# Attention scores in two one-bank tiles, and three banks in place of four for transposes

## The chip, the cores and the metric

The kernel runs on one core of one Trainium2 chip. The metric is the time in microseconds on the device for one execution, the median of several runs. Engines are named as the profile names them: PE is TensorE's matmul side and PEld its weight loads, DVE is VectorE, ACT is ScalarE, POOL is GpSimd, SP is SyncE, whose queue issues most transfers. [...]

## What is computed

Sparse attention, and behind it a routed layer of eight experts on its output. Of the eight heads, the first four look back over 32 positions (local), the last four at positions of the same remainder by 32 (strided). Cut to what matters:

```python
def _attn_ref(q, k, v):                 # 8 batches, 8 heads, 576 positions, 64 wide
    scores = scale * np.matmul(q, k.transpose(0, 1, 3, 2))
    mask_local = (rel >= 0) & (rel < stride)
    mask_strided = (rel >= 0) & (pos[None, :] % stride == pos[:, None] % stride)
    scores = np.where(masks[None, :, :, :], scores, -1000000000.0)
    scores = scores - np.max(scores, axis=-1, keepdims=True)
    attn = np.exp(scores)
    attn = attn / (np.sum(attn, axis=-1, keepdims=True) + 1e-09)
    return np.matmul(attn, v)

def _moe_ref(x, w_skip, w_gate, w1, w2):   # x: attention output, 4608 rows of 512
    do_compute = x @ w_skip > 0
    e_idx = np.argmax(x @ w_gate, axis=1)  # for the rows with do_compute
    y = gate_w * (np.maximum(x @ w1[e], 0.0) @ w2[e])
    out = x + y where do_compute, else x
```

All inputs and the output are float32.

## The kernel before

**Stages.** The first part, up to about 178 us, is the attention of all batches, with the routing of each finished batch woven in. The second part is the expert layers: weights are loaded and split in two parts, rows are gathered, and three matmuls stand for each float32 product. The second part opens PSUM pools of its own; the edit touches only the pool of the first.

**Units.** A batch is four units of attention (`UNITS`): two local ones of 5 and 4 blocks (64 queries against 96 keys each) and two strided ones of 6 and 5 blocks (54 queries against 54 keys, in tiles of 64). Two pairs of heads, j = 0 and 1, are done together, and each pair's two heads lie in the lower and upper 64 partitions, i = 0 and 1. A score matmul takes 64 rows of the array and writes 64 partitions, so the four combinations of i and j use the four 64x64 tiles of the array: row half i, column half i xor j.

**The steps of a unit.** `qk` (line 189) multiplies the scores into a tile tagged "S" (line 199), DVE adds the mask into an SBUF buffer `sm` (line 206 local, 208 strided), takes the maxima (214), and POOL subtracts them, one instruction for each j (217). The two strided units share one `sm` buffer. `tex` (222) transposes the result on PE in groups of up to four into a bank tagged "T" (237), and ACT's Exp copies each group out (245). `pv` (251) multiplies by the values into a two-bank tile "PV" (271), and DVE normalises (279 to 286). `xpose` (304) transposes the unit's output in groups of four into T banks (313), and ACT copies them to `xT` (315). There is one `xT` buffer for each kind of head, shared by all batches.

**The routing of a batch.** `score` (325) multiplies `xT` with the router's weights in two halves, each in a T bank (329), which ACT empties with two copies (333, 334). `route1` (337) transposes that into a T bank (349), and DVE works out the choice; `route2` (396) counts ranks in a T bank (400 to 406), read at 411; `place` (452) multiplies one-hot matrices into a T bank (456), read at 460 or 462.

**What sets the order.** One loop over the 32 units (line 848). In visit n it runs the scores of unit n + 2, then the transposes of unit n's exponentials, pv of unit n - 1, and the output transposes of unit n - 2. The orders of PE, DVE and POOL in this loop are those of the program text (`manual_schedule`, line 847); ACT and the transfers are ordered by the framework's scheduler. In the visit of a batch's first strided unit the loop puts `xpose` of the same batch's first local unit ahead of pv, and after pv come `score` half 0, `score` half 1 of the batch before, and then `tex` (lines 874 and 903). In the visit of the next batch's first local unit come `tex`, pv, `route2`, `xpose`, and `place` (lines 887 to 908).

**PSUM.** The pool of the first part gives out eight banks by tag: S one tile of two banks, T four tiles of one, PV one tile of two. A tile is given out anew when the instructions that read it are through.

## Time and profile before

| | us |
|---|---|
| median of 3 runs | 451.05 |
| lowest and highest | 447.95, 451.74 |
| the profiled execution, its own time | 453.04 |
| its span, first to last instruction | 451.3 |
| mean granted TensorE clock in it | 0.976 |

The profile is of one execution, so sums over its rows are to be held against 453.04 and not against the median. A row of the timeline gives start and length in us, engine, line, operation, the tiles out and in, the shape, and in brackets how long the engine sat idle before it and what ended that. A row may stand for several instructions (x40); a matmul in float32 makes two records. PE's records overlap, since matmuls are pipelined, so a row's length is the start times of its matmuls and the length of the last.

### The profile page before, as it was taken

The numbers are of one execution on the slowest core, as the hardware profiler recorded it, in microseconds if no ns is written. First come the engines' busy times: TensorE is split into PE (matmuls) and PEld (weight loads), VectorE is DVE, ScalarE is ACT, GpSimd is POOL, SyncE is SP. The second block draws the span as 40 slices with busy tenths as digits, with TensorE's granted clock in tenths as the row PEclk, the third lists the DMA queues.
The fourth block names the chain that finished last, engine by engine and source line by source line (L and its number), as shares of the span: only waits on it lengthen the run. The fifth ranks groups of instructions, "written<-read, shape, count | busy, mean of one in ns | idle before, by whom it ended". The sixth has DMA issues, their size and how long they took to land.

```text
span 451.3 us, 12196 instructions
## 1 busy us (share of the span) xinstructions
PE 412.4 (91%) x4991; PEld 370.0 (82%) x4992; DVE 280.9 (62%) x606; ACT 186.4 (41%) x370; POOL 142.6 (32%) x200
## 2 busy tenths in 40 slices
PE   5989899799889667999899999999999999999994
PEld 3866768587677556789799799999999999999984
DVE  2666798969987876781377465365484564755611
ACT  1334443436345316642443243444444444544400
POOL 2434445344454355034014327012224023200201
PEclk9799999999989979999999999999999999999999
DMA  8999989979893134515347466546566466655201
GB/s 287 388 393 315 350 276 343 326 227 352 265 377 120 43 101 153 172 69 141 91 155 212 155 201 205 167 153 187 187 199 186 152 209 192 210 159 169 61 20 42
DMA packets 51805, 90.38 MB, mean 200 GB/s; under 512 B 8251, under 2 KB 27963, under 8 KB 51745
## 3 DMA queue, kind: packets, MB, share of 16 engines
q1 hardware_dynamic: 45249, 79.19, 52.8%
q0 software_dynamic: 6496, 10.37, 8.0%
q8 instruction: 40, 0.66, 0.6%
q14 instruction: 20, 0.16, 0.1%
HBM read 75.16 MB, written 14.91 MB: 200 GB/s over the span
## 4 chain that ended last, share of the span: by engine, by line
PE 50%; DMA 2%; POOL 0%; DVE 0%; POOLq 0%; issue 0%
PE S L652 15%; PE S L654 15%; PE S L653 15%; PE PV L744 2%; DMA xg<-out_dram,tab 2%; PE T L646 1%; PE PV L786 0%; PE PV L784 0%; PE PV L785 0%; PE S L760 0%; PE S L759 0%; PE S L761 0%; POOL out_dram L732 0%; PE T L771 0%; PE S L646 0%; PE PV L646 0%
## 5 line engine op out<-in xcount | busy, mean ns | idle before, releaser
L652 PE MATMUL S<-xh,w1h 128*128 128x342 f32 (+6 forms) x248 | 78.6, 317 | 0.2 <-DVE hl L665 0.2
L654 PE MATMUL S<-xh,w1l 128*128 128x342 f32 (+6 forms) x248 | 76.7, 309 | 0.0
L653 PE MATMUL S<-xl,w1h 128*128 128x342 f32 (+6 forms) x248 | 76.6, 309 | 0.0
L732 POOL DMA_INDIRECT out_dram<-ot,tab x25 | 28.0, 1122 | 150.0 <-DVE ot L730 141.8
L652 PE MATMUL S<-hh,w2h 128*128 128x288 f32 (+5 forms) x192 | 59.4, 310 | 0.5 <-DVE hl L665 0.5
L654 PE MATMUL S<-hh,w2l 128*128 128x288 f32 (+5 forms) x192 | 58.0, 302 | 0.0
L653 PE MATMUL S<-hl,w2h 128*128 128x288 f32 (+5 forms) x192 | 57.9, 302 | 0.0
L664 ACT ACTIVATE hh<-S 128x342 fp32r<-128x342 f32 (+6 forms) x64 | 28.0, 437 | 64.0 <-PE S L654 58.3
L588 DVE TENSOR_TENSOR w1l<-raw,w1h 128x1024 fp32r<-128x1024 f32 x32 | 39.0, 1223 | 20.0 <-ACT w1h L582 20.0
L199 PE MATMUL S<-kt,qt 64*64 64x54 f32 (+1 forms) x1280 | 34.3, 247 | 14.9 <-DVE sms L208 5.0
L652 PEld LDWEIGHTS S<-xh,w1h 128*128 128x128 f32 x248 | 46.9, 189 | 0.9 <-issue 0.4
L653 PEld LDWEIGHTS S<-xl,w1h 128*128 128x128 f32 x248 | 46.8, 189 | 0.1
L654 PEld LDWEIGHTS S<-xh,w1l 128*128 128x128 f32 x248 | 46.7, 188 | 0.0
L199 PEld LDWEIGHTS S<-kt,qt 64*64 64x64 f32 x1280 | 28.3, 145 | 22.2 <-issue 7.3
L217 POOL TENSOR_TENSOR sm<-sm,mx 128x480 f32<-128x480 f32 (+1 forms) x32 | 28.5, 911 | 55.8 <-DVE mx L214 29.3
L624 POOL DMA_INDIRECT xg<-out_dram,tab x25 | 33.7, 1347 | 36.8 <-issue 14.4
L588 DVE TENSOR_TENSOR w2l<-raw,w2h 128x1024 fp32r<-128x1024 f32 x32 | 39.1, 1223 | 9.8 <-ACT w2h L582 9.6
L665 DVE SCALAR_TENSOR_TENSOR hl<-S,hh 128x342 fp32r<-128x342 f32 (+6 forms) x64 | 30.9, 483 | 17.8 <-ACT hh L664 17.7
L652 PEld LDWEIGHTS S<-hh,w2h 128*128 128x128 f32 x192 | 36.1, 188 | 0.8 <-DVE hl L665 0.8
L315 ACT COPY xT<-T 128x512 f32<-128x512 f32 (+4 forms) x56 | 22.2, 441 | 35.0 <-PE T L313 34.8
L649 DVE TENSOR_TENSOR xl<-T,xh 128x288 fp32r<-128x288 f32 (+7 forms) x30 | 13.1, 468 | 37.3 <-ACT xh L648 37.2
L653 PEld LDWEIGHTS S<-hl,w2h 128*128 128x128 f32 x192 | 36.3, 189 | 0.0
(180 smaller groups left out, 828.3 us busy)
## 6 DMA issues: line engine op xcount, KB each, us to landing
raw<-in_w_dram SPq DMA_DIRECT2D x64, 512.0 KB
vt<-in_vp_dram SPq DMA_DIRECT2D x40, 390.0 KB
qt<-in_qp_dram SPq DMA_DIRECT2D x16, 304.0 KB
kt<-in_kp_dram SPq DMA_DIRECT2D x16, 297.0 KB
out_dram<-x SPq DMA_DIRECT2D x16, 288.0 KB
kt<-in_kp_dram SPq DMA_DIRECT2D x14, 304.0 KB
qt<-in_qp_dram SPq DMA_DIRECT2D x14, 288.0 KB
out_dram<-x SPq DMA_DIRECT2D x32, 99.0 KB
```

The source lines that it names most:

```text
L199: T.matmul(s[HP * (i ^ j):HP * (i ^ j) + HP, j, (blk - b0) * win:(blk - b0 + 1) * win], lhsT=qt[p, j, blk * nq:blk * nq + HP], rhs=kt[p, j ...
L217: G.tensor_tensor(e[:, j], sw[:, j], mx[:, j].unsqueeze(2).broadcast_to([128, b1 - b0, win]), op=ALU.subtract)
L315: A.copy(xT_[b, kind][:, :, g * nq:(g + m) * nq].rearrange("p i (n q) -> p n i q", q=nq), t[:, 0:m * 128].rearrange("p (n i q) -> p n i q" ...
L588: V.tensor_tensor(lo, raw_.pop((key, j)), hi.bitcast(F32), op=ALU.subtract)
L624: i = G.indirect_dma_start(out=xg[:s["P"], t, :], out_offset=None, in_=out[0:last, :], in_offset=bass.IndirectOffsetOnAxis(ap=s["tab"][:s[ ...
L649: V.tensor_tensor(xl[:, c, :C], t[:, :C], xh[:, c, :C].bitcast(F32), op=ALU.subtract)
L652: T.matmul(p, lhsT=a[0], rhs=b[0], start=start, stop=False)
L653: T.matmul(p, lhsT=a[0], rhs=b[1], start=False, stop=False)
L654: T.matmul(p, lhsT=a[1], rhs=b[0], start=False, stop=stop)
L664: A.activation(s["hh"][:, f, :C], p[:, :C], AF.Relu)
L665: V.scalar_tensor_tensor(s["hl"][:, f, :C], p[:, :C], 0.0, s["hh"][:, f, :C].bitcast(F32), op0=ALU.max, op1=ALU.subtract)
L732: i = G.indirect_dma_start(out=out, in_=ot[:P], in_offset=None, bounds_check=NTOK - 1, oob_is_err=False, out_offset=bass.IndirectOffsetOnA ...
```

## The change

The score tile of two banks becomes two tiles of one bank, taken one after the other from three that carry the tag S; T has three banks in place of four. The loop over the matmuls is turned round: first all blocks for j = 0, then all for j = 1. The mask is added by two instructions, one for each tile, each half as long. What follows (maxima, subtraction, and all else) is as it was, and so is the number of matmuls.

```diff
-    psum, bufs = pctx.enter_context(tc.tile_pool(name="psum", bufs=1, space=PSUM)), {"S": 1, "T": 4, "PV": 1}
+    psum, bufs = pctx.enter_context(tc.tile_pool(name="psum", bufs=1, space=PSUM)), {"S": 3, "T": 3, "PV": 1}
...
-        s = ps("S", 2)
-        for blk in range(b0, b1):
-            for j in range(2):
+        s = [None, None]
+        for j in range(2):
+            s[j] = ps("S")
+            for blk in range(b0, b1):
                 for i in range(2):
                     p = slice(HP * i, HP * i + HP)
-                    T.matmul(s[HP * (i ^ j):HP * (i ^ j) + HP, j, (blk - b0) * win:(blk - b0 + 1) * win],
+                    T.matmul(s[j][HP * (i ^ j):HP * (i ^ j) + HP, (blk - b0) * win:(blk - b0 + 1) * win],
                              lhsT=qt[p, j, blk * nq:blk * nq + HP], rhs=kt[p, j, blk * nq:blk * nq + win],
                              start=True, stop=True)
         yield
         sm = sms[pr][:, :, 0:n]
-        if kind == 0:
-            mask = con["ml"][:, (b0 > 0) * LW:(b0 > 0) * LW + n]
-            V.tensor_tensor(sm, s[:, :, 0:n], mask.unsqueeze(1).broadcast_to([128, 2, n]), op=ALU.add)
-        else:
-            V.tensor_tensor(sm.rearrange("p j (n w) -> p j n w", w=win),
-                            s[:, :, 0:n].rearrange("p j (n w) -> p j n w", w=win),
-                            con["ms"].unsqueeze(1).unsqueeze(1).broadcast_to([128, 2, b1 - b0, win]), op=ALU.add)
+        for j in range(2):
+            if kind == 0:
+                mask = con["ml"][:, (b0 > 0) * LW:(b0 > 0) * LW + n]
+                V.tensor_tensor(sm[:, j], s[j][:, 0:n], mask, op=ALU.add)
+            else:
+                V.tensor_tensor(sm[:, j].rearrange("p (n w) -> p n w", w=win),
+                                s[j][:, 0:n].rearrange("p (n w) -> p n w", w=win),
+                                con["ms"].unsqueeze(1).broadcast_to([128, b1 - b0, win]), op=ALU.add)
```

## The prediction

> **What bounds the kernel now.** I read the page first (busy shares, slices, the chain that ended last), then the windows view of the attention part, then the waits, and then the timeline where the edited tiles are used.

> ```profile
> span 451.3 us, 12196 instructions
> PE 412.4 (91%) x4991; PEld 370.0 (82%) x4992; DVE 280.9 (62%) x606; ACT 186.4 (41%) x370; POOL 142.6 (32%) x200
> PE   5989899799889667999899999999999999999994
> DVE  2666798969987876781377465365484564755611
> DMA  8999989979893134515347466546566466655201
> PE 50%; DMA 2%; POOL 0%; DVE 0%; POOLq 0%; issue 0%
> ...
> 20.00:147.00 127.00, 113.65 (x2514) 90.78 (x2506) 101.95 (x267) 57.84 (x136) 56.23 (x98) 0.97 0.90 306
> ```

> The last row is the windows view from 20 to 147 us: busy time of PE, PEld, DVE, ACT and POOL, then the granted clock, the DMA share and GB/s. PE is busy 113.65 of 127 us, so it idles 13.4 us; DVE is busy 80%, ACT 46%, and the DMA engines 0.90. The chain that ended last runs on PE. What delays PE in the attention part (about the first 178 us) therefore delays the end, unless a later wait takes the delay up. Nothing after that part uses the edited pools. The profiled execution took 453.04 us (span 451.3, 1.7 around it); the median shown is 451.05, 2.0 lower. I sum on 453.04 and take 2.0 off.

> **What the third score bank can give.** In the old kernel the scores of the next unit cannot start before the mask of the last one has emptied the only buffer. These are PE's waits for it, in total and at their places:

> ```profile
> PE S L199 <- DVE sms L208: 5.0, 5, 1.8
> PE S L199 <- DVE sm L206: 2.1, 2, 1.1
> PE S L199 <- DMA kt<-in_kp_dram: 3.9, 5, 2.6
> ...
> 11.62 0.46 PE L199 MATMUL S<-kt,qt 64*64 64x54 f32 x4 [1.06 <-DVE sm L206]
> 12.33 1.53 PE L199 MATMUL S<-kt,qt 64*64 64x54 f32 x44 [0.25 <-DMA kt<-in_kp_dram]
> ...
> 51.64 0.38 PE L199 MATMUL S<-kt,qt 64*64 64x54 f32 x9 [0.68 <-DVE sms L208]
> 56.35 0.41 PE L199 MATMUL S<-kt,qt 64*64 64x96 f32 x6 [0.68 <-DVE sms L208]
> 112.12 0.80 PE L199 MATMUL S<-kt,qt 64*64 64x54 f32 x40 [0.43 <-DVE sms L208]
> 117.58 0.41 PE L199 MATMUL S<-kt,qt 64*64 64x96 f32 x4 [1.46 <-DVE sms L208]
> 151.01 0.27 PE L199 MATMUL S<-kt,qt 64*64 64x54 f32 x2 [1.00 <-DVE sm L206]
> 157.35 0.34 PE L199 MATMUL S<-kt,qt 64*64 64x54 f32 x8 [1.78 <-DVE sms L208]
> 164.07 0.36 PE L456 MATMUL T<-hpm,hlo 128*128 128x120 bf16 x2 [3.58 <-POOL hpm L446]
> ```

> With three one-bank tiles a unit's first tile always finds a bank that the unit before last has left, and its second needs only the first half of the last unit's mask. I let all mask waits go: 7.1 us by the first two rows. Of these 0.68 + 0.68 + 0.43 + 1.46 = 3.25 lie where PE goes on afterwards. The 1.00 and 1.78 do not count: at 164.07 PE waits 3.58 us more, for a POOL product at the end of a chain of DVE and POOL work, so an earlier PE only waits longer there. The 1.06 at 11.62 I cost at nothing: a load of kt is late next, at 12.33. The gain is 3.3 us; its ends are 0 and 7.1.

> **What the fourth transpose bank was worth: the two score products of the router.** Once a batch (first visit of its strided half), PE does in order: two groups of transposes of the new outputs (L313), pv, `score` half 0, `score` half 1 (L329), then `tex` (L237). Each group and each half takes a bank of T:

> ```profile
> 76.95 0.74 PE L313 MATMUL T<-cs,x 128*128 128x128 f32 x5
> 78.61 2.11 PE L329 MATMUL T<-xT,w 128*64 128x288 f32 x16
> 79.85 0.39 ACT L333 COPY s<-T 32x288 f32<-32x288 f32 x1 [3.29 <-PE T L329]
> 80.26 0.65 ACT L334 COPY s<-T 32x288 f32<-32x288 f32 x1
> 80.93 0.76 ACT L315 COPY xT<-T 128x512 f32<-128x512 f32 x2
> 81.01 1.00 PE L237 MATMUL T<-cs,frame 128*118 128x128 f32 x6 [0.29 <-issue]
> ```

> The copies of the transposes (L315) do not run when the transposes are done at 77.69, although ACT then sits idle for 3.29 us: they write `xT`, of which there is one buffer, and `score` of the batch before still reads it. So two banks stay held until both halves are multiplied. With four banks the halves take the other two, and only `tex` waits: it starts at 81.01, just behind half 0's copies (80.91). With three, half 1 has no bank left and waits itself for those copies. Half 0 takes half of the 16 records' start times, about 0.9 us, so half 1 could start at 79.5 and starts at 81.0: 1.45 us. Then all three banks hang on half 1. Its first `xT` copy can follow about 1.24 us after its start (78.61 to 79.85 is the same distance), at 82.2, and takes some 0.52 of the 0.76 for two; `tex` starts at 82.75 in place of 81.01. That is 1.74 us, less 0.1 that the second `tex` group waits today: 1.65 us. This happens for six batches alike (the seventh runs its halves before its transposes: 0.5 us). The sum is 6 x 1.65 + 0.5 = 10.4 us. Below, if `tex` is not hurt again, 6 x 1.45 less today's wait of 0.5 each = 5.7; above, if ACT does half 1's copies (0.39 + 0.65) before the `xT` copies, 6 x 2.4 = 14.4. Nothing covers it: PE's order is written out by hand, and the next unit's scores stand behind `tex`.

> **The placing product.** The second place where four banks are in use at once:

> ```profile
> 70.62 0.19 PE L400 MATMUL T<-rohb,tri 128*128 128x40 bf16 x1
> 70.78 0.85 PE L313 MATMUL T<-cs,x 128*128 128x128 f32 x6
> 71.47 0.43 PE L456 MATMUL T<-hpm,hlo 128*128 128x120 bf16 x5
> 71.51 0.76 ACT L315 COPY xT<-T 128x432 f32<-128x432 f32 x2 [0.88 <-PE T L313]
> 71.83 0.80 PE L199 MATMUL S<-kt,qt 64*64 64x54 f32 x40
> 72.09 0.19 DVE L411 TENSOR_TENSOR rdd<-T,rohb 128x40 f32<-128x40 f32 x1
> ```

> The ranks (L400) hold a bank until DVE reads them at 72.09, the two groups of L313 hold two, and `place` (L456) needs a fourth at 71.47. With three it waits for the first copy, which ends near 72.05: 0.6 us, in four batches, 2.4 us (ends 0 and 4 x 0.8 for the read at 72.28). Elsewhere (the `tex` groups of a local unit, `route1`) I find three banks enough: a bank is copied out before its third successor starts.

> **The new order of the score matmuls.** The old loop visits all four 64x64 tiles of the array in every block; the new one does all blocks on two tiles (j = 0), then all on the other two. Each matmul makes two records.

> ```profile
> 69.77 0.92 PE L271 MATMUL PV<-vt,pts 54*64 54x65 f32 x40
> ...
> 95.52 1.39 PE L271 MATMUL PV<-vt,ptl 96*64 96x65 f32 x40
> 97.53 1.06 PE L199 MATMUL S<-kt,qt 64*64 64x96 f32 x40
> ```

> Taking off a last matmul of 0.22 to 0.24 us, the old order gives one record in 21 ns (96 columns) and, by the row at 71.83, in 15 ns (54 columns). If only two tiles ran at a time it would be about 42 and 30 ns; the local pv, which has only two tiles, shows 30 ns at 65 columns. That costs 0.83 + 0.67 + 0.70 + 0.58 = 2.8 us a batch, 22 us in all. But the strided pv (69.77) also orders its work by pairs, four matmuls on the two tiles of one half of the rows and then four on those of the other, and still runs at 18 ns: PE started the other tiles while earlier work of the first two was pending. So the order need not be kept between tiles, over at least four matmuls. Here the distance is 8 to 12. Ends: 0 and 22 us. I take 1.6 us (0.05 for each of 32 units, the time to step over the first tile's work), because the pv row is the nearest.

> [...]

> **The split mask.** One DVE instruction becomes two of half the length.

> ```profile
> L206 DVE TENSOR_TENSOR sm<-S,cs 128x960 f32<-128x960 f32 x8 | 9.2, 1150 | 6.7 <-DMA cs<-in_cst_dram 6.4 <-PE S L199 0.3
> L206 DVE TENSOR_TENSOR sm<-S,cs 128x768 f32<-128x768 f32 x8 | 7.6, 951 | 2.2 <-PE S L199 2.2
> L208 DVE TENSOR_TENSOR sms<-S,cs 128x540 f32<-128x540 f32 x8 | 5.7, 714 | 9.8 <-POOL frame L217 8.3 <-PE T L313 1.5
> ```

> From 768 to 960 elements costs 199 ns, so about 155 ns of each are fixed: 32 more of them are 5.0 us of DVE. In 20 to 147 us DVE has 25 us idle, which hides it; behind a mask stand the normalising of pv, the maxima and POOL's subtraction. Where DVE is late already (147 to 164 us), four units pay 0.15 each: 0.6 us, ends 0 and 5. Against it, the masks that wait for POOL (8.3 us in the last row, off PE's path) can now start their first half after POOL's first subtraction; I cost that at nothing.

> **The sum**: -3.3 + 10.4 + 2.4 + 1.6 + 0.6 = +11.7 us. Of PE's 13.4 us of idle time, waits that the profile calls "issue" and loads can shrink when PE comes later; I take 1.7 off for them. 453.04 + 10.0 = 463.0, and for the median 461.

> **The rivals.**
> 1. Two tiles at a time (strict order): 22 in place of 1.6 us: 481; with a view ahead that covers half of it, 470. For it: nothing here shows a distance of 8 to 12. Against it: the row at 69.77. Chance 0.12 for the full price, 0.10 for half.
> 2. Something else paces the attention part, so that the bank waits fill idle time that was there anyway: 13.4 us of it, as much as the sum. For it: the DMA share of 0.90. Against it: PE waits only 3.9 us for kt loads, in five places. Time: 451 to 452. Chance 0.16.
> 3. Faster: half 1 of `score` does not wait, because the `xT` copies can be done before it. The 10.4 then becomes 0 (and today's 0.5 a batch goes too, 3.0), and the mask waits decide: 451 - 7.1 - 3.0 + 2.4 + 1.6 + 0.6 = 445.5. It decides if the copies of L315 start before the second half of L329. Against it: ACT's idle 3.29 us. Chance 0.08.

> **How the numbers follow.** My forecast has chance 0.54, its own range 455 to 468: the ends of the `score` term (5.7, 14.4) and of the gain (0, 7.1). The range of all is 450 to 476: it takes in rival 2 and half the price of rival 1 and leaves out rival 3 and the full price. Within 1% (446.5 to 455.6) is what a measurement of this kernel can hardly tell from no change. Faster: 0.08. Same: rival 2 and 0.04 of the forecast's lower end, 0.20. Slower: 0.72.

> **What would show it.** Right: the 16 records of L329 split in two eights about 1.45 us apart, PE waiting for ACT's L334 between them, and `tex` (L237) some 4.2 us after the start of L329 (2.4 now); no wait of L199 for L206 or L208; score runs of 40 records near 0.85 and 1.1 us; L456 behind the first L315. Wrong: runs of 1.4 to 1.9 us (rival 1); PE idle in 20 to 147 us unchanged and the same span (rival 2); L315 ahead of the second half of L329 (rival 3).

## The result, and the profile after

The changed kernel takes 466.6 us (median of 4 runs, 465.1 to 469.0) beside 450.5 us for the kernel before on the same chip: a ratio of 1.037, 95% interval 1.030 to 1.044. It is slower by some 16 us. Its profiled execution took 467.75 us with a span of 466.0 us.

Lines are one or two further down in the changed kernel: `score` is L331 (L329 before), its copies L335 and L336, `tex` L239, the output transposes L315 with their copies L317, `place` L458, the scores of a unit L200. First the page (span, busy times, PE's slices):

```profile
span 466.0 us, 12240 instructions
PE 425.1 (91%) x4991; PEld 382.6 (82%) x4992; DVE 284.7 (61%) x638; ACT 187.2 (40%) x370; POOL 142.7 (31%) x200
PE   7888989898979868699899999999999999999994
```

And the windows view from 20 to 147 us, in the columns of the row shown of before:

```profile
20.00:147.00 127.00, 111.59 (x2306) 91.12 (x2303) 95.00 (x269) 51.90 (x124) 49.84 (x88) 0.99 0.89 299
```

PE has as many records in all as before (4991), but in the same 127 us it gets through 2306 of them where it did 2514. It idles more (15.4 us in place of 13.4), and it is also busy for longer with the same matmuls: 425.1 us in the whole span against 412.4. Both have to be explained. The loss lies in the attention part alone: the router's last score product starts at 199.91 us where it started at 185.53, so 14.4 of the 14.7 us of span are there by then.

The waits of PE in the changed kernel (total us, times, longest), by size:

```profile
PE T L331 <- ACT s L336: 7.2, 6, 1.2
PE T L239 <- ACT xT L317: 4.9, 6, 0.8
PE T L458 <- POOL hpm L448: 4.0, 1, 4.0
...
PE T L458 <- ACT xT L317: 1.3, 3, 0.4
...
PE T L239 <- ACT ptl L247: 0.7, 1, 0.7
PE S L200 <- DVE sms L210: 0.7, 1, 0.7
```

The first two are new: six times PE waits for ACT ahead of the second half of `score`, and six times for the copy of the output transposes ahead of `tex`. The waits for a mask (5.0 and 2.1 us before) have shrunk to 0.7. In the timeline, one of the places of `place` and then one of the six of `score`:

```profile
75.66 0.85 PE L315 MATMUL T<-cs,x 128*128 128x128 f32 x6
...
76.38 0.76 ACT L317 COPY xT<-T 128x432 f32<-128x432 f32 x2 [0.88 <-PE T L315]
...
76.96 0.44 PE L458 MATMUL T<-hpm,hlo 128*128 128x120 bf16 x5 [0.45 <-ACT xT L317]
...
84.68 1.14 PE L331 MATMUL T<-xT,w 128*64 128x288 f32 x8
...
85.92 0.39 ACT L335 COPY s<-T 32x288 f32<-32x288 f32 x1 [3.78 <-PE T L331]
...
86.33 0.64 ACT L336 COPY s<-T 32x288 f32<-32x288 f32 x1
87.03 1.19 PE L331 MATMUL T<-xT,w 128*64 128x288 f32 x8 [1.21 <-ACT s L336]
...
88.30 0.75 ACT L317 COPY xT<-T 128x512 f32<-128x512 f32 x2 [1.33 <-PE T L331]
...
89.03 1.50 PE L239 MATMUL T<-cs,frame 128*118 128x128 f32 x6 [0.81 <-ACT xT L317]
```

`place` waits 0.45 us for the first copy of the transposes just ahead of it. Half 1 of `score` starts at 87.03, behind the second copy of half 0 (86.33 + 0.64). ACT then waits in its turn for half 1, since only then may `xT` be overwritten, and `tex` waits for that copy. From the first score record to `tex` it is 4.35 us (89.03 less 84.68); before it was 2.40 (81.01 less 78.61). Seen from the end: PE, ACT, PE, ACT, PE, each waiting for the last.

The score matmuls of the four kinds of unit, one row for each (start, length, count), strided at 54 columns and local at 96:

```profile
122.27 1.19 PE L200 MATMUL S<-kt,qt 64*64 64x54 f32 x40
...
126.41 1.60 PE L200 MATMUL S<-kt,qt 64*64 64x96 f32 x40
...
135.35 1.27 PE L200 MATMUL S<-kt,qt 64*64 64x96 f32 x32
...
139.28 1.43 PE L200 MATMUL S<-kt,qt 64*64 64x54 f32 x48
```

The 40 records of a local unit took 1.06 us before and take 1.60. Taking off the last matmul's 0.24 us, that is 35 ns a record in place of 21. From the first start to the last, the units of 40 and 32 local and of 48 and 40 strided records are 0.54, 0.38, 0.51 and 0.39 us longer where nothing interrupts them, 1.82 together or 14.6 for eight batches (14.8 in the expectations below). The page's group of this line (busy us, mean ns of one, idle time before it) shows it too:

```profile
L200 PE MATMUL S<-kt,qt 64*64 64x54 f32 (+1 forms) x1280 | 47.0, 240 | 4.1 <-DMA kt<-in_kp_dram 2.0
```

Before, the same group had 34.3 us busy, with 14.9 us of idle time in front of it. The order of the matmuls has made the score work itself longer.

### The profile page after: what moved, and what is told of

Same layout as the page of the kernel before. It is cut to its first block, busy times and chain, and to the rows that moved or that the text cites. A ratio compares the mean times of both kernels' runs of the same rounds, so it can differ in the third digit from the quotient of the medians.

```text
span 466.0 us, 12240 instructions
## 1 busy us (share of the span) xinstructions
PE 425.1 (91%) x4991; PEld 382.6 (82%) x4992; DVE 284.7 (61%) x638; ACT 187.2 (40%) x370; POOL 142.7 (31%) x200
## 4 chain that ended last, share of the span: by engine, by line
PE 49%; DMA 1%; POOL 0%; DVE 0%; POOLq 0%; issue 0%
PE S L654 14%; PE S L656 14%; PE S L655 14%; PE PV L746 2%; PE T L648 1%; DMA xg<-out_dram,tab 1%; PE PV L788 0%; PE PV L786 0%; PE PV L787 0%; PE S L762 0%; PE S L761 0%; PE S L763 0%; POOL out_dram L734 0%; PE T L773 0%; PE S L648 0%; PE PV L648 0%
## 5 line engine op out<-in xcount | busy, mean ns | idle before, releaser
L200 PE MATMUL S<-kt,qt 64*64 64x54 f32 (+1 forms) x1280 | 47.0, 240 | 4.1 <-DMA kt<-in_kp_dram 2.0
L200 PEld LDWEIGHTS S<-kt,qt 64*64 64x64 f32 x1280 | 41.8, 138 | 10.2 <-issue 5.4
L317 ACT COPY xT<-T 128x512 f32<-128x512 f32 (+4 forms) x56 | 22.2, 441 | 42.0 <-PE T L315 33.9
L656 PEld LDWEIGHTS S<-hh,w2l 128*128 128x128 f32 x192 | 36.3, 189 | 0.0
```

Of the source, the lines that this page charges most:

```text
L200: T.matmul(s[j][HP * (i ^ j):HP * (i ^ j) + HP, (blk - b0) * win:(blk - b0 + 1) * win], lhsT=qt[p, j, blk * nq:blk * nq + HP], rhs=kt[p, j ...
L317: A.copy(xT_[b, kind][:, :, g * nq:(g + m) * nq].rearrange("p i (n q) -> p n i q", q=nq), t[:, 0:m * 128].rearrange("p (n i q) -> p n i q" ...
L656: T.matmul(p, lhsT=a[1], rhs=b[0], start=False, stop=stop)
```

## The experiments

**First set: which part costs.** Theory 1 held the lost T bank and the new order of the matmuls both for costly, theory 2 the order alone, theory 3 the lost T bank alone. Four kernels lie between the old one and the new. In their comparison the kernel before had 450.8 us.

Only the fourth T bank is taken away; its place stays empty:

```diff
-{"S": 1, "T": 4, "PV": 1}
+{"S": 1, "T": 3, "PV": 1}
```

> The old kernel with one bank less for T (three) and nothing else changed; the eighth bank stays empty. Theory 1 (bank waits and matmul order each cost PE time, both real): the waits at the router's halves cost what the changed kernel shows there, 4.35 us from the first L329 to tex in place of 2.41, 1.94 us in six batches, and 0.6 us at place in four: 14 us of PE time, of which up to 5 fill idle time that was there: 460 to 465 us. Theory 2 (the matmul order costs everything, bank waits fill idle time): 450 to 452. Theory 3 (bank waits cost everything): 466.

Measured: 462.4 us (461.4 to 465.0), ratio 1.029, interval 1.024 to 1.034. That is 11.6 of the 16 us, with nothing else changed. The waits of PE from 38 to 175 us, in this kernel:

```profile
PE T L329 <- ACT s L334: 7.2, 6, 1.2
PE T L237 <- ACT xT L315: 4.9, 6, 0.8
...
PE T L456 <- ACT xT L315: 1.8, 4, 0.5
PE S L199 <- DVE sms L208: 1.1, 1, 1.1
```

The same circle stands here at the same size. The last row matters too: the waits for the strided mask, 5.0 us in the kernel before, are down to 1.1 although there is still one score tile. A PE that waits for ACT comes later to the next scores and finds the mask done.

The change with the old order of matmuls, and the change with two S banks and four T banks:

```diff
-        s = [None, None]
-        for j in range(2):
-            s[j] = ps("S")
-            for blk in range(b0, b1):
+        s = [ps("S"), ps("S")]
+        for blk in range(b0, b1):
+            for j in range(2):
```

> The changed kernel with the score matmuls in the old order (block by block, all four tiles of the array in turn), on two one-bank tiles taken beforehand; banks 3 and 3 as in the change. Theory 1: runs of 40 score records are 0.82 and 1.05 us again in place of 1.2 and 1.6, so the 14.8 us of PE time that the new order costs go, less some idle time that comes back: 453 to 456 us. Theory 2 (order is all): 450 to 452 or less. Theory 3 (bank waits are all): 465 to 467.

```diff
-{"S": 3, "T": 3, "PV": 1}
+{"S": 2, "T": 4, "PV": 1}
```

> The changed kernel with banks S 2 and T 4 in place of 3 and 3: new matmul order and split mask, no third score bank, no T lost. Theory 1: the halves of score run on as before, the order's 14.8 us stay, and the mask waits come back in part (a unit's first tile waits for the first half of the last mask): 458 to 465 us. Theory 2: 466 or more. Theory 3: 451.

Both edits together:

> Only the split mask and two one-bank tiles in place of one two-bank tile: old matmul order, S 2 and T 4. Theory 1: DVE's 4 to 5 us more lie beside PE's work: 449 to 453 us. Rival (the split mask is what hurts, since DVE's work is in line with PE's): 455 or more.

| S banks, T banks, order | us | ratio, interval |
|---|---|---|
| one tile of 2, T 3, old order | 462.4 | 1.029, 1.024 to 1.034 |
| 3, T 3, old order | 464.4 | 1.033, 1.028 to 1.037 |
| 3, T 3, new order (the change) | 466.6 | 1.037, 1.030 to 1.044 |
| 2, T 4, new order | 453.4 | 1.007, 1.004 to 1.011 |
| 2, T 4, old order | 450.4 | 0.998, 0.994 to 1.001 |

With four T banks nearly all of the loss is gone. The new order costs 3.0 us with four T banks (453.4 less 450.4, intervals apart) and 2.2 with three (464.4 to 466.6, intervals that overlap). The third S bank, together with the split mask, shows no gain while T has three: 464.4 beside 462.4, with intervals that overlap. So theory 2 falls. Theory 1 gave the first of these times (460 to 465) and missed the next two (453 to 456 and 458 to 465), for it held the order for costly. Theory 3 is nearly right, but for the order's few us.

**Second set: the circle taken apart, first attempt.** If the loss is the circle of transposes, score and copies, moving the steps against each other must undo it with three banks. Here both halves of `score` go ahead of the transposes, and so ahead of pv, in six batches:

```diff
         if len(front) > 1:
+            if b > 0 and pr == 2:
+                run(score(b - 1, 0), score(b - 1, 1))
             run(seq.pop(0))
...
-        if b > 0 and pr == 2:
+        if b > 0 and pr == 2 and n + LA >= len(units):
             seq = [score(b - 1, 0), score(b - 1, 1)] + seq
```

It was tried on four of the kernels above; the times without the move in the table below are those of the first set.

> Old score tile of two banks and old order, three transpose banks; in six batches both halves of the router's score product now stand before the two transpose groups instead of behind them. Theory A (the loss is one circle: the transpose groups hold two banks until score is through, and score needs two): the waits of PE for ACT behind the first half (7.2 us) and before the exponentials' transposes (4.9 us) go almost wholly, and the time falls from 462.4 to 450 to 453. Theory B (three banks are too few anywhere, and the wait moves to the next user): new waits for ACT of 6 us or more stand before the second transpose group or the next tile, and the time stays at 458 or above.

> Three one-bank score tiles with split masks, the old order of the score matmuls, three transpose banks, score before the transposes in six batches. Theory A: 464.4 less 12 is 452. On the third score bank, beside the run with the old two-bank tile and the same move: if the mask waits were worth what the prediction took (3.3 us), this one is 3 us faster than that; if they only fill time that PE would have waited anyway, the two agree within 1.5 us.

> The changed kernel, with score before the transposes in six batches and nothing else. Theory A: 466.6 less 12 is 454 to 455, so that the new order of the score matmuls, 2 to 3 us, is what is left of the loss. Theory B: 460 or above. A third possibility, that with the bank waits gone PE has no idle time left into which the 14.8 us of longer score work can go: 458 to 464, with waits of PE for ACT gone all the same.

> Two one-bank score tiles with split masks, old order, four transpose banks, score before the transposes in six batches. Theory A: even with four banks tex waited about 0.5 us a batch for a bank, which goes: 447 to 449, against 450.4 with score behind. If that wait was hidden, or the earlier score waits for the last outputs' copies instead: 450 to 452.

| kernel | without the move | with it | ratio to before (450.2), interval |
|---|---|---|---|
| one S tile of 2, T 3, old order | 462.4 | 457.3 | 1.015, 1.008 to 1.021 |
| S 3, T 3, old order | 464.4 | 454.7 | 1.010, 1.007 to 1.014 |
| the change | 466.6 | 459.1 | 1.017, 1.010 to 1.025 |
| S 2, T 4, old order | 450.4 | 455.0 | 1.010, 1.006 to 1.013 |

Neither theory A nor theory B had this: theory A's 12 us were not met (5.1, 9.7 and 7.5), theory B's waits for ACT do not come, and with four banks the move costs 4.6 us (intervals apart). The third possibility, named for the changed kernel alone, has its time (458 to 464); that PE has no idle time left there is not shown. The first kernel of the table shows why theory A failed. Its waits of PE from 38 to 175 us:

```profile
PE S L199 <- DVE sm L206: 9.2, 5, 2.1
...
PE T L237 <- ACT s L334: 0.5, 1, 0.5
```

And its timeline on PE and DVE, at one of the five places:

```profile
80.90 1.15 PE L271 MATMUL PV<-vt,ptl 96*64 96x65 f32 x32
...
82.10 0.17 DVE L279 TENSOR_SCALAR rc<-PV 128x8 f32<-128x8 f32 x1 [2.35 <-PE PV L271]
...
87.42 0.95 DVE L206 TENSOR_TENSOR sm<-S,cs 128x768 f32<-128x768 f32 x1
...
88.43 1.08 PE L199 MATMUL S<-kt,qt 64*64 64x54 f32 x48 [2.02 <-DVE sm L206]
```

The 12.1 us of T waits are gone (0.5 are left), and 9.2 us for a mask have come. With `score` ahead of it, pv stands later in PE's order. DVE, whose order is fixed too, has the normalising of that pv at its head and stands idle for 2.35 us; all that is behind it comes late, the next mask (87.42) among it, and PE, which needs the score tile, waits 2.02 us. In this kernel the price of a T bank has become, by its waits, the price of a late pv. With three one-bank S tiles part of that is spared: in the second kernel these waits are 5.9 us, and it is 2.6 us faster than the first. The expectation was 3 us if the third bank has the worth that the prediction gave it, and within 1.5 if not; the intervals overlap, so this stays undecided. The changed kernel with the move stays 4.4 us above the same kernel with the old order (459.1, 454.7; overlapping again), so the order may cost more once PE waits less.

**Third set: the circle taken apart without a late pv.** pv keeps its place or comes earlier; behind it the two halves of `score`, then the transposes, then `tex`:

```diff
-        if len(front) > 1:
+        if len(front) > 1 and not (g and pr == 2):
             run(seq.pop(0))
```

> Three one-bank score tiles with split masks, old order of the score matmuls, three transpose banks; in six batches PE does pv first, then the two score halves, then the two transpose groups, then tex. Theory C (two things cost: PE's wait for a transpose bank, and a pv that comes later, for whose normalising DVE then holds up the next mask): pv comes earlier than ever, half 1 has a bank at once, and tex waits some 0.6 us a batch for half 1's copies. 464.4 less about 7 to 9 is 455 to 457; if the normalising that now comes earlier also spares mask waits, 452 to 454. Theory B (three banks are short in any order): 460 or above.

> The same order of pv, score and transposes with two one-bank score tiles and four transpose banks. Theory C: tex finds a bank some 0.3 us earlier and pv comes 0.8 us earlier in six batches, 447 to 449.5 against 450.4 without the move; and it lies well under the 455.0 of the version with score ahead of pv. If pv's place is not what cost there: 453 or above, since score's own place is as late as before only for the transposes.

With S 3, T 3 and the old order: 454.1 us (451.4 to 458.1), ratio 1.010, interval 1.007 to 1.014, so 10.3 us of the 464.4 are undone by the move of one step. Theory C's first range (455 to 457) is just missed and its second (452 to 454) just about met, but not for the reason given with it: the waits for a mask went only from 2.1 to 1.6 us. Two of its waits of PE from 38 to 175 us, and its timeline at the place:

```profile
PE T L238 <- issue: 3.4, 5, 0.7
...
PE T L457 <- ACT xT L316: 1.7, 4, 0.5
...
81.44 2.11 PE L330 MATMUL T<-xT,w 128*64 128x288 f32 x16
...
83.47 0.76 PE L314 MATMUL T<-cs,x 128*128 128x128 f32 x5
...
84.19 0.64 ACT L335 COPY s<-T 32x288 f32<-32x288 f32 x1
...
84.85 0.76 ACT L316 COPY xT<-T 128x512 f32<-128x512 f32 x2
...
84.93 1.00 PE L238 MATMUL T<-cs,frame 128*118 128x128 f32 x6 [0.69 <-issue]
```

The 16 records of `score` run through in 2.11 us, and from their start to `tex` it is 3.49 us with the transposes (0.76) now among them; in the changed kernel it was 4.35 without them. The three banks are the same in number. It is the order in which they are taken and given back that cost 10 us. What is left of the wait stands at `tex`, which starts just behind half 1's second copy (84.19 + 0.64 = 84.83). With S 2 and T 4 the same move gives 451.4 us, ratio 1.002, interval 0.999 to 1.006, against 450.4 without it. The wait of `tex` with four banks, put at 0.5 us a batch in the prediction, is 1.7 us over six batches in that kernel's waits and 1.2 with the move, so there was little to win, and the 447 to 449.5 of theory C is missed. As theory C has it, this lies under the 455.0 of the version with a late pv. With three S and three T banks, though, the late pv shows no price: 454.7 with it and 454.1 without, while the waits for the local mask are 5.9 us in the one and 0.4 in the other. So only with four T banks do the times show that a late pv costs.

**Why the new order costs so little.** PE's score work is 12.7 us longer by its busy time (14.6 by the starts), but the time only 2 to 3 us. Either the split mask hides that, because its first half can start early, or PE has idle time into which the work goes. The kernel before with nothing but the order turned:

```diff
-        for blk in range(b0, b1):
-            for j in range(2):
+        for j in range(2):
+            for blk in range(b0, b1):
```

> The kernel before with nothing changed but the order of the score matmuls: one two-bank score tile, one mask, four transpose banks, all blocks of j = 0 and then all of j = 1. The question is why 14.8 us more of score work on PE cost only 3 us with two one-bank tiles. Theory D (the first half's mask can start while PE does the second half, so that DVE is not held up, and PE only works where it waited): here DVE gets its scores 0.4 to 0.55 us later in each of 28 units, and the time is 459 to 465. Theory E (PE has idle time enough for it in any case, wherever the mask starts): 452 to 454, as with the split mask.

Measured: 453.1 us (451.2 to 456.3), ratio 1.008, interval 1.004 to 1.012. That is theory E's time and not theory D's: the mask's split is not what hides it. The windows row of this kernel:

```profile
20.00:147.00 127.00, 120.07 (x2490) 98.85 (x2494) 101.14 (x264) 58.75 (x137) 56.55 (x98) 1.00 0.90 308
```

And its waits of PE from 38 to 175 us:

```profile
PE S L199 <- DVE sms L208: 2.6, 5, 1.2
...
PE S L199 <- issue: 0.9, 1, 0.9
```

PE is busy 120.07 us where it was 113.65, and gets through 2490 records where it did 2514: its idle time has halved, from 13.4 to 6.9 us, and the work has gone on almost as fast. Waits for a mask have become longer score runs (5.0 to 2.6 us, and 3.3 to 0.9 of the "issue" waits ahead of the scores in the same stretch). Score work that grew where PE would have waited cost little time here (2.9 us); that is the reading, and it rests on these totals.

Idle time does not pay for all of it. In this window the score matmuls take 9.1 us longer (35.04 us for 992 records, 25.97 for 1010 before). PE's idle time is 6.4 us less, and all else on PE takes 2.7 us less, with 6 records fewer, at a granted clock of 1.00 in place of 0.97. Over the runs, the mean clock of this kernel is 0.987 and that of the kernel before, beside it, 0.977. What the clock is worth in the time, and whether it is higher because PE idles less, was not measured.

**How far PE looks ahead between tiles of the array.** With four T banks and two S banks, the blocks of a unit were taken in chunks: a chunk's j = 0, then its j = 1, then the next, with another chunk in each batch:

```diff
-        s = [None, None]
-        for j in range(2):
-            s[j] = ps("S")
-            for blk in range(b0, b1):
+        s = [ps("S"), ps("S")]
+        step = (1, 1, 2, 2, 3, 4, 5, 6)[b]
+        for c0 in range(b0, b1, step):
+            for j, blk in [(j, blk) for j in range(2) for blk in range(c0, min(c0 + step, b1))]:
```

> Two one-bank score tiles, split masks, four transpose banks; the score matmuls go by chunks of blocks: a chunk's j = 0, then its j = 1, then the next chunk. The chunk is 1 block in the first two batches, 2 in the third and fourth, then 3, 4, 5 and 6. Theory F (PE starts work on the other two tiles of the array when no more than three pairs of records of the first two are still to start): ns per record at five blocks of 96 columns 21, 23, 27, 31 and 35 for chunks of 1, 2, 3, 4 and 5, and at six blocks of 54 columns 15, 16, 19, 21, 24 and 26 for 1 to 6. Strict order: 21, 31, 35, 37 and 39 and 15, 23, 25, 27, 28 and 29. A look-ahead over 40 and more records: 21 and 15 throughout. Time between 450 and 454.

One execution took 451.2 us, inside the expected 450 to 454. The rows of its score matmuls, local ones of 40 with chunks of 1, 2, 4 and 5, then strided ones of 48 with 2, 4, 5 and 6:

```profile
19.56 1.06 PE L200 MATMUL S<-kt,qt 64*64 64x96 f32 x40
...
35.97 1.11 PE L200 MATMUL S<-kt,qt 64*64 64x96 f32 x40
...
95.25 1.44 PE L200 MATMUL S<-kt,qt 64*64 64x96 f32 x40
...
115.46 1.60 PE L200 MATMUL S<-kt,qt 64*64 64x96 f32 x40 [1.21 <-DVE sms L210]
...
45.65 0.96 PE L200 MATMUL S<-kt,qt 64*64 64x54 f32 x48
...
105.56 1.19 PE L200 MATMUL S<-kt,qt 64*64 64x54 f32 x48
...
126.00 1.31 PE L200 MATMUL S<-kt,qt 64*64 64x54 f32 x48
...
148.95 1.43 PE L200 MATMUL S<-kt,qt 64*64 64x54 f32 x48 [0.61 <-DVE sm L208]
```

Less 0.24 us for the last matmul, over 39 and 47 distances: 21, 22, 31 and 35 ns a record, and 15, 20, 23 and 25. Theory F gave 21, 23, 31, 35 and 16, 21, 24, 26. Strict order gave 21, 31, 37, 39 and 23, 27, 28, 29. The chunk of three took 1.61 us in its first unit, at 73.33, which is 35 ns where theory F gave 27; but the second tile's bank was being read by a mask until 73.84, so this unit says nothing on the order. The 32 records of the same batch at 80.16 had no such wait and took 1.10 us, 28 ns. Some other units of 40 at 54 columns are not used either: there the second tile's bank was still being read by a mask.

## Why the prediction was right or wrong

**Right: the direction, its place and its mechanism.** The fourth T bank decides. Half 1 of `score` starts 2.35 us behind half 0 (84.68, 87.03), where 0.9 were taken for the kernel before: the 1.45 us of the prediction. `tex` follows 4.35 us after the start, where "some 4.2" was said. The two terms for the bank were 10.4 and 2.4 us, together 12.8; the run that takes the bank alone away gives 11.6. Of these, `place` was put at 0.6 in each of four batches; its waits in that run are 1.8 us over four. Rival 3 (half 1 does not wait) is out. That "three banks are enough" elsewhere held but for one `tex` wait of 0.7 us.

**Wrong: the gain of the third S bank, -3.3 us.** The step took PE's waits for a mask where "PE goes on afterwards" as saved. But the two edits were summed as if they did not touch. Once PE waits for ACT, it comes late to the next scores and most waits for the strided mask are gone with no third bank (5.0 to 1.1 us with the one T bank less). The third bank with the split mask, at three T banks and the old order, stands at 464.4 beside 462.4, where the prediction's two terms (-3.3 and +0.6) come to -2.7. This is 4.7 of the 5.6 us by which 461 was missed; the 1.7 taken off for waits that shrink is not seen as a gain of its own, since the measured parts hold it already; the T bank's 1.2 less than 12.8 and the order's 0.6 more make up the rest to 0.2 (4.7 + 1.7 - 1.2 + 0.6 = 5.8).

**Right for the wrong reason: the order of the matmuls, +1.6 us.** The size was near (2.2 and 3.0, and 2.9 in the kernel before). The step was wrong: PE was said to look ahead over 8 to 12 matmuls so that a score run of 40 records stays at 0.85 and 1.1 us. It takes 1.19 and 1.60; the distance found is three pairs of records. No run shows the 0.05 us a unit of which the term is made: the four kinds of unit are longer by 0.38 to 0.54 us. Two thirds of rival 1's full price lie in PE's work (1.82 us a batch from the four kinds of unit, of 2.8), but not in the time, and that the term came out near 1.6 is luck. Rival 1 was in part right on PE's work and wrong on the end; rival 2 (it fills time that was idle anyway) was in the main right for this term, apart from what the clock may have paid, and wrong for the bank.

**The split mask** adds 3.8 us to DVE's busy time (280.9 to 284.7, 32 more instructions), where 5.0 were worked out. What it costs in time was not measured by itself; two one-bank tiles with split masks at four T banks are no slower than before (0.998, 0.994 to 1.001).

**Open.** With the circle taken apart, the kernel with three T banks still takes 1.0% more than before (0.7 to 1.4). `place` keeps waits of 1.7 us there, and `tex` waits 3.4 us in five places where it waited 1.4 before; together that is 3.7 of the some 4 us, but that these waits are what is left was not tested. The granted clock differs between the kernels as well: on the mean of the runs it is 0.976 before, 0.967 with only the T bank taken away and 0.982 in the change. Whether it follows from PE's waits, and how much of each difference it makes, is open. The price of the third S bank apart from the split mask at three T banks is open too. Three S banks together with four T banks and the two of PV would be nine, one more than the pool gives out in any kernel here, and were not tried. No version was found that beats the kernel before.

## What to carry to other kernels

Count banks by when they are given back, not by how many tiles are in use: a bank whose copy must wait for a later product, which itself needs a bank of the same tag, closes a circle, and a move of one step in the order can be worth more than a bank (here 10.3 us, where the third S bank showed no gain). Do not add up the gain and the loss of two edits that act on the same engine in turn: the wait that one edit makes may cover the wait that the other saves. And when a step is moved ahead, look at what it pushes back, on the other engines too.
